# Pooled attention and Strassen feed-forward on one core: in the first unit, three copies of q of batch 1 one slot earlier, its scores and three turned parts one slot later

## The chip, the cores and the metric

The kernel runs on one core of one Trainium2 chip, all in float32. Its time is the device time of one execution in microseconds (us); of several runs the median is given. "The profile" is a page on one execution taken by the hardware profiler, and "the trace" is the record of every instruction of that execution, of which parts are shown. A chip core has five engines with a queue of instructions each, which run in order within a queue and wait for each other by semaphores: TensorE (PE in the profile, its weight loads PEld), VectorE (DVE), ScalarE (ACT), GpSimd (POOL) and SyncE (SP, which here only issues DMAs). ACT also issues a few DMAs (ACTq).

## The reference: what is computed

Two stages. First attention over 8 batches, 8 heads, 576 rows of 64, with k and v averaged over groups of 8 rows, so that there are only 72 keys:

```python
k_p = k.reshape(B, H, Sp, pool, D).mean(axis=3)
v_p = v.reshape(B, H, Sp, pool, D).mean(axis=3)
scores = scale * np.matmul(q, k_p.transpose(0, 1, 3, 2))
attn = softmax(scores)
x = (attn @ v_p), heads side by side: 4608 tokens of 512
h = x @ w_in                       # 512 -> 2048
g = h + sin(alpha * h) ** 2 / alpha
out = g @ w_out                    # 2048 -> 512
```

## The kernel before, in words

**Units and slots.** The first half of the feed-forward (x to g) is done for 9 units of 512 tokens; a batch of attention has 576 rows, so batch b+1 must be ready, in part, for unit b+1. While a unit's large products run on PE, the attention of the next batch is woven in between. `run` (L1476) calls for every unit u first `carry(u)` (L1164), which makes a dictionary from slot numbers to lists of small steps, and then `hidden(u, x)` (L814), which walks through 28 slots: four groups J = 0 to 3 of 7 slots each, k = 0 to 6. A slot issues one of the seven products of a Strassen scheme (`product`, L834; eight PE instructions on 256 columns at L842), the copies, sines and squares that go with it, and, at the place `extras()`, the steps that `carry` has put there, in the order in which they were put. No scheduler moves anything: the order of the text is the order in each engine's queue.

**What a slot of unit 0 issues** (with J its group, Q the group before):

- k = 0: last sines of Q, extras, product 1 into bank `b1`
- k = 1: ACT copies `b1` to `b6` (L818), squares of Q (L999), extras, product 5 into `b5`
- k = 2: VectorE sums of Q (`finish`, L1044), extras, product 6 into `b6`
- k = 3: store of g of Q (L1058), ACT copies `b6` to `b7` and `b5` to `p5` (L818), extras, product 2 into `b1`
- k = 4: first sines of J out of `b1` and their squares on ACT (L992, L999), extras, product 7 into `b7`
- k = 5: VectorE sum of `b7` and `p5` (L817), extras, product 3 into `b6`
- k = 6: VectorE sums (L817) and sines, extras, product 4 into `b7`

**The attention steps of batch 1 in unit 0.** q of batch 1 comes by DMA into the tile `q0`. `pairs_q` (L87) copies its five row tiles on ACT (L97) into the tile `q1`, with the heads in another order. `q_t(i)` (L279) turns row tile i: four transposes on PE (L287) into one bank and one copy out (L288), on VectorE for i = 0 and 1, on ACT for 2 to 4, into the tile `q0` again, which is free for this only when all five copies of `pairs_q` have read it. `k_t` (L271) turns the pooled keys (L276) and copies them to `kblk` on VectorE (L277). `two_scores(j)` (L301) multiplies turned q by keys (L315): for j = 0 row tiles 0 and 1, for j = 1 row tiles 2, 3 and 4; VectorE takes maximum and difference of them (`shifts`, L338 and L339), of row tile 3 and 4 only later, in slot 13 (`two_shifts`). `exp(i)` is on ACT (L364), `norm(i)` sums on VectorE (L370, L371) and multiplies on POOL (L372), `turn(i)` transposes blocks on VectorE (L499 to L509), and `move` (L512) brings the turned weights by DMA (L519) from `tr` to `aM`, of which SP issues twelve and ACT four. `all_values` (slot 26, L598) multiplies them by the pooled values. `norm_rest`, `a_rest` (L485, its copy L491) and `values_rest` (L585, L591) do the same for the last 64 rows of batch 0.

**What binds these steps besides data.** PSUM has 8 banks. Five of them (0 to 4) rotate through the groups: a group takes four, so at any time one is free, and `two_scores` uses that one, `(turn + 1) % 5`, and the banks 5, 6 and 7 beside it. The turning steps take their banks in rotation out of 5, 6 and 7 (`abank`, L772): in unit 0 the bank 6 for `q_t(0)`, 7 for `q_t(1)`, 5 for `k_t`, then 6, 7 and 5 for `q_t(2)`, `q_t(3)` and `q_t(4)`. `two_scores` puts the scores of its first row tile into the free bank and bank 7, those of the second (with those of tile 4) into banks 5 and 6. `load_q(2)` (slot 9, L69) loads batch 2 into the tile `q1`, out of which `q_t(0)` to `q_t(4)` read. Sines and exponentials need different function tables on ACT (ACT_TABLE_LOAD).

**POOL in unit 0.** `combine_w_in` (L679, adds at L683) makes the Strassen sums of the first weights for group J; `load_v(1)` (slot 7) adds up rows of v (L131) once its DMA has landed, then come `combine_w_in(2)` (slot 8), `norm(0)` and `norm(1)` (slot 10), `norm_rest` (slot 13), `norm(2)` and `norm(3)` (slot 16), `combine_w_in(3)` (slot 17).

After the 9 units, `outputs` (L1273) does the second half of the feed-forward in the same manner; nothing in it is touched.

Of the kernel before, what the change touches and what calls it, by code (L numbers as in the profile page):

```python
# [40 lines left out]
class Kernel:  # L41
# [1122 lines left out]
    def carry(self, u):  # L1164

        nc = self.nc
        x = defaultdict(list)
        at = lambda slot, f, *a: x[slot].append(lambda: f(*a))
        last = self.B - 1
        b = u + 1  # L1170
        if u == 0:
            A0, A = self.att[:2]
            at(1, A0.rest_q)
            at(1, A0.a_head, 1, (5, 6, 2))
            at(1, self.refine)
            at(2, A0.values, (2, 3), (2, 1), 1, 1)
            at(2, A0.score, 4)
            at(2, self.sums_of_x, 0, 2)
            at(2, self.sums_of_x, 0, 3)
            at(2, self.load_w_in_part, 2)  # L1180
            at(2, self.load_w_in_part, 3)
            at(2, self.pairs_q, 1, (0, 1))
            at(4, self.pairs_q, 1, (2, 3, 4))
            at(4, self.combine_w_in, 1, (0, 1, 2, 3), self.nc.gpsimd)
            at(4, A.q_t, 0, self.nc.vector.tensor_copy)
            at(4, A.q_t, 1, self.nc.vector.tensor_copy)
            at(4, A.k_t)
            at(7, self.load_v, 1)
            at(7, lambda: self.pool_v())
            for i in range(2):  # L1190
                at((5, 10)[i], A.two_scores, i)
            at(13, A.two_shifts)
            for i in range(2, 5):
                at(5 + i, A.q_t, i)
            at(9, A0.exp, 4)
            for i in range(4):
                at((9, 9, 15, 15)[i], A.exp, i)
                at((10, 10, 16, 16)[i], A.norm, i)
                at((13, 13, 19, 19)[i], A.turn, i)
            at(8, self.combine_w_in, 2, (0, 1, 2, 3), self.nc.gpsimd)  # L1200
            at(13, A0.norm_rest)
            at(17, self.combine_w_in, 3, (0, 1), self.nc.gpsimd)
            at(17, self.combine_w_in, 3, (2, 3), self.nc.gpsimd)
            at(23, A0.a_rest)
            at(24, lambda: A0.values_rest((5, 6, 7, (self.turn + 1) % 5)))
            for r in (32, 96):
                at(3, self.nc.gpsimd.memset, self.aM[r:r + 32, :, 704:736], 0.0)
            at(19, A.move, range(3))
            at(20, A.move, (3,), nc.scalar, (0,))
            at(21, A.move, (3,), nc.scalar, (1,))  # L1210
            at(26, A.all_values)
            at(9, self.load_q, 2)
            at(23, self.inner_w_in)
            for e in range(2):
                at(12, self.load_k, 2, e)
                at(17, lambda e=e: self.pool_k[e]())
            at(27, self.att[2].k_t)
            turn = 23
        else:
            at(0, self.sums_of_x, u, 2)  # L1220
            at(0, self.sums_of_x, u, 3)
        if 0 < u < last:
            A = self.att[b]
            for i in range(2):
                at((3, 5)[i], A.two_scores, i)
            at(6, A.two_shifts)
            for i in range(4):
                at((8, 9, 10, 10)[i], A.exp, i)
                at((9, 10, 11, 12)[i], A.norm, i)
                at((12, 13, 13, 13)[i], A.turn, i)  # L1230
            at(14, A.move, range(4))
            at(6, self.load_v, b)
            at(12, lambda: self.pool_v())
            for i in range(2):
                if b < last:
                    at(12, self.load_k, b + 1, i)
                    at(12, lambda i=i: self.pool_k[i]())
            at(25, A.all_values)
            if b < last:
                at(26, self.att[b + 1].k_t)  # L1240
            if 2 < u + 2 <= last:
                at(7, self.load_q, u + 2)
            at(2, self.inner_x, u)
            turn = 22
        elif u:
            turn = None
        if turn and u + 2 <= last:
            for part in range(4):
                at(((turn, turn + 1) if u == 0 else (23, 24))[part] if part < 2 else turn + part, self.turn_q, u + 2, part)
        if u + 1 < self.NU:  # L1250
            at(27, self.sums_of_x, u + 1, 0)
            at(27, self.sums_of_x, u + 1, 1)
        return x
# [336 lines left out]
```

## Time and profile before

| | |
|---|---|
| median of 3 runs (lowest to highest) | 908.77 us (908.37 to 908.81) |
| profiled execution, its own time | 905.98 us |
| its span, first to last instruction | 904.2 us |
| busy share PE, PEld, DVE, ACT, POOL | 99%, 90%, 75%, 50%, 23% |
| granted TensorE clock, mean | 0.999 |

The views that are used: the page (busy time by engine, the chain of work that ended last), the timeline of one engine (start, duration, engine, line, operation, output<-inputs, tile, xcount of merged instructions; in square brackets the idle time of the engine just before it and what ended it), the list of waits (who waited for whom: total us, times, longest) and the groups by form (mean ns of one shape). Times in a timeline are us from the span's start. Starts of merged instructions can overlap the one before, as engines are pipelined.

### The profile page before, as it was taken

The numbers are of one execution on the slowest core, as the hardware profiler recorded it, in microseconds if no ns is written. First come the engines' busy times: TensorE is split into PE (matmuls) and PEld (weight loads), VectorE is DVE, ScalarE is ACT, GpSimd is POOL, SyncE is SP. The second block draws the span as 40 slices with busy tenths as digits, with TensorE's granted clock in tenths as the row PEclk, the third lists the DMA queues.
The fourth block names the chain that finished last, engine by engine and source line by source line (L and its number), as shares of the span: only waits on it lengthen the run. The fifth ranks groups of instructions, "written<-read, shape, count | busy, mean of one in ns | idle before, by whom it ended". The sixth has DMA issues, their size and how long they took to land.

```text
span 904.2 us, 17920 instructions
## 1 busy us (share of the span) xinstructions
PE 894.7 (99%) x7002; PEld 815.3 (90%) x7002; DVE 677.6 (75%) x1012; ACT 448.6 (50%) x1072; POOL 212.1 (23%) x216
## 2 busy tenths in 40 slices
PE   9899999999999999999999999999999999999998
PEld 5687888888888888888888999999999999999997
DVE  7675766758577685764557799979798888889895
ACT  5596785877768777687976621111111111111111
POOL 5687552824438253330000000000000000000000
PEclk9999999999999999999999999999999999999999
DMA  9965866759577595648217246161618162533401
GB/s 262 246 199 148 212 175 192 193 146 277 144 208 189 167 247 138 180 132 307 85 67 239 96 135 211 47 203 40 223 27 227 36 189 74 171 92 123 141 14 40
DMA packets 128746, 141.12 MB, mean 156 GB/s; under 512 B 46920, under 2 KB 95704, under 8 KB 128664
## 3 DMA queue, kind: packets, MB, share of 16 engines
q1 hardware_dynamic: 125880, 137.88, 53.2%
q10 hardware_dynamic: 2784, 2.11, 0.9%
q8 instruction: 55, 0.90, 0.4%
q14 instruction: 27, 0.22, 0.1%
HBM read 75.37 MB, written 47.19 MB: 136 GB/s over the span
## 4 chain that ended last, share of the span: by engine, by line
PE 95%; DVE 2%; SPq 1%; ACT 1%; DMA 1%; issue 0%; DVEq 0%
PE PS L842 44%; PE PS L1323 41%; PE PS L1022 3%; PE PS L315 2%; PE PS L608 2%; SPq L677 1%; PE PS L621 1%; DVE x L1278 1%; DMA a<-in_moe_w_in_dram 1%; PE PS L1090 0%; DVE s L1278 0%; DVE r L1278 0%; PE PS L420 0%; PE PS L276 0%; SPq L101 0%
## 5 line engine op out<-in xcount | busy, mean ns | idle before, releaser
L842 PE MATMUL PS<-home,a 128*128 128x256 f32 x1104 | 257.8, 381 | 0.2
L842 PEld LDWEIGHTS PS<-home,a 128*128 128x128 f32 x1104 | 205.3, 190 | 32.6 <-issue 4.5
L842 PE MATMUL PS<-home,as 128*128 128x256 f32 x768 | 183.0, 382 | 0.0
L842 PEld LDWEIGHTS PS<-home,as 128*128 128x128 f32 x768 | 141.6, 190 | 19.8 <-ACT PS L818 1.2
L1373 POOL TENSOR_TENSOR cc<-cc,cb 128x576 f32<-128x576 f32 x1 | 2.0, 1982 | 501.8 <-DVE cb L1278 501.8
L1323 PE MATMUL PS<-s,wb 128*128 128x144 f32 x896 | 119.1, 286 | 0.0
L1323 PEld LDWEIGHTS PS<-s,wb 128*128 128x128 f32 x896 | 113.7, 190 | 0.1
L999 ACT ACTIVATE s<-s,c 128x256 f32<-128x256 f32 (+1 forms) x228 | 113.5, 564 | 0.0
L817 DVE TENSOR_TENSOR h<-PS,p 128x512 f32<-128x512 f32 x72 | 49.1, 683 | 64.4 <-PE PS L842 38.1
L131 POOL TENSOR_TENSOR kvin<-kvin 96x768 f32<-96x768 f32 (+3 forms) x42 | 74.6, 1776 | 71.4 <-DMA kvin<-in_v_dram 69.7
L1451 ACT COPY PS<-PS 128x144 f32<-128x144 f32 x56 | 14.7, 263 | 144.8 <-PE PS L1323 140.7
L992 ACT ACTIVATE s<-h,al 128x256 f32<-128x256 f32 x144 | 65.6, 509 | 41.7 <-DVE h L817 41.7
L1323 PE MATMUL PS<-r,wb 128*128 128x144 f32 x512 | 73.3, 286 | 0.3 <-DVE r L1278 0.3
L1323 PE MATMUL PS<-s,a 128*128 128x144 f32 x512 | 73.2, 286 | 0.0
L1044 DVE TENSOR_TENSOR h<-PS,s 128x512 f32<-128x512 f32 x36 | 24.7, 686 | 60.2 <-ACT s L999 60.2
L992 ACT ACTIVATE s<-PS,al 128x256 f32<-128x256 f32 x144 | 60.1, 470 | 18.7 <-PE PS L842 17.8
L1323 PEld LDWEIGHTS PS<-r,wb 128*128 128x128 f32 x512 | 67.1, 190 | 0.5 <-DVE r L1278 0.5
L1323 PEld LDWEIGHTS PS<-s,a 128*128 128x128 f32 x512 | 67.1, 190 | 0.0
L818 ACT COPY PS<-PS 128x512 f32<-128x512 f32 x72 | 41.4, 576 | 35.1 <-PE PS L842 30.3
L1471 ACT COPY PS<-PS 128x144 f32<-128x144 f32 x56 | 14.7, 263 | 88.1 <-PE PS L1323 88.1
L1323 PE MATMUL PS<-s,we 128*128 128x144 f32 x384 | 54.9, 286 | 0.0
L1323 PE MATMUL PS<-x,wb 128*128 128x144 f32 x384 | 54.9, 286 | 0.0
(216 smaller groups left out, 1406.1 us busy)
## 6 DMA issues: line engine op xcount, KB each, us to landing
g_bridge<-h SPq DMA_DIRECT2D x72, 512.0 KB
r<-g_bridge SPq DMA_DIRECT2D x31, 1152.0 KB
out_dram<-o SPq DMA_DIRECT2D x122, 72.0 KB
kvin<-in_k_dram SPq DMA_DIRECT2D x14, 576.0 KB
q<-in_q_dram SPq DMA_DIRECT2D x7, 1024.0 KB
kvin<-in_v_dram SPq DMA_DIRECT2D x14, 512.0 KB
aM<-tr SPq DMA_DIRECT2D x54, 92.0 KB
aM<-tr SPq DMA_DIRECT2D x54, 88.0 KB
```

Of the source, the lines that this page charges most:

```text
L131: self.nc.gpsimd.tensor_tensor(out=t[..., 0:w] if w > D else out, in0=t[..., 0:w], in1=t[..., w:2 * w], op=OP.add)
L315: nc.tensor.matmul(ps[e][r0 + r:r0 + r + q.shape[-1], h, :], q[s], kb[s, hp, :], start=True, stop=True)
L608: nc.tensor.matmul(o[r:r + 64], w, x, start=start and i < 2, stop=False, skip_group_check=True)
L817: add = lambda o, x, y: nc.vector.tensor_tensor(out=o, in0=x, in1=y, op=OP.add)
L818: copy = lambda o, x: nc.scalar.copy(out=o, in_=x)
L842: nc.tensor.matmul(ps[:, jj, :], self.A[p][:, kk, f * P:(f + 1) * P], x[:, kk, :], start=(start and n == 0), stop=(kk == 1), skip_group_ch ...
L992: self.nc.scalar.activation(out=G.s[:, i, jj, j, :], in_=src[:, jj], func=AF.Sin, scale=self.al[:, f:f + 1])
L999: self.nc.scalar.activation(out=x, in_=x, func=AF.Square, scale=self.c[:, f:f + 1])
L1022: nc.tensor.matmul(o, W[m][:, G.J - J0], X[m], start=start and n == 0, stop=True, skip_group_check=True)
L1044: add = lambda o, x, y: self.nc.vector.tensor_tensor(out=o, in0=x, in1=y, op=OP.add)
L1323: nc.tensor.matmul(out, W[:, J // 2, J % 2, :], A[:, J, :], start=(start and J == 0), stop=(J == self.NJ - 1), skip_group_check=True)
L1451: nc.scalar.copy(out=x1[:, 0, :], in_=x0[:, 1, :])
```

## The change

In unit 0 only, in `carry`. `pairs_q` for row tiles 2, 3 and 4 goes from slot 4 to slot 3. In slot 4 it stood behind the first sines and squares of group 0 on ACT; in slot 3 it stands behind the two copies L818 and ahead of those sines, and ahead of two memsets of POOL. `two_scores(0)` goes from slot 5 to 6 and `two_scores(1)` from 10 to 11. `q_t(2)`, `q_t(3)` and `q_t(4)` go from slots 7, 8 and 9 to 8, 9 and 10. The exponentials of row tiles 0 and 1 (slot 9), the norms (slot 10) and `load_q(2)` (slot 9) stay; so `q_t(4)` now stands behind the exponentials and behind `load_q(2)`, and the norms of tiles 0 and 1 ahead of `two_scores(1)`.

```diff
             at(2, self.pairs_q, 1, (0, 1))
-            at(4, self.pairs_q, 1, (2, 3, 4))
+            at(3, self.pairs_q, 1, (2, 3, 4))
             at(4, self.combine_w_in, 1, (0, 1, 2, 3), self.nc.gpsimd)
             at(4, A.q_t, 0, self.nc.vector.tensor_copy)
             at(4, A.q_t, 1, self.nc.vector.tensor_copy)
...
             for i in range(2):
-                at((5, 10)[i], A.two_scores, i)
+                at((6, 11)[i], A.two_scores, i)
             at(13, A.two_shifts)
             for i in range(2, 5):
-                at(5 + i, A.q_t, i)
+                at(6 + i, A.q_t, i)
             at(9, A0.exp, 4)
```

## The prediction

> **What bounds the kernel now.** I read the page first, its busy row and its chain:
>
> ```profile
> PE 894.7 (99%) x7002; PEld 815.3 (90%) x7002; DVE 677.6 (75%) x1012; ACT 448.6 (50%) x1072; POOL 212.1 (23%) x216
> ...
> PE 95%; DVE 2%; SPq 1%; ACT 1%; DMA 1%; issue 0%; DVEq 0%
> ```
>
> PE is busy for 99% of the span and carries 95% of the chain that ended last. So an edit in unit 0 gains only what PE stands idle there, and the gain lasts only if PE doesn't have to wait for something else further down. I therefore read the timeline of PE through unit 0, and then those of the engines that PE waits for. PE (start, duration, instructions, idle time before):
>
> ```profile
> 33.06 1.92 PE L842 MATMUL PS<-home,a 128*128 128x256 f32 x8
> 37.49 1.23 PE L315 MATMUL PS<-kblk,q 64*64 64x72 f32 x64 [2.51 <-DVE kblk L277]
> 38.65 1.99 PE L842 MATMUL PS<-home,as 128*128 128x256 f32 x8
> 40.48 1.89 PE L842 MATMUL PS<-home,a 128*128 128x256 f32 x8
> 42.21 0.60 PE L287 MATMUL PS<-ident,q 128*128 128x128 f32 x4
> 42.64 1.89 PE L842 MATMUL PS<-home,a 128*128 128x256 f32 x8
> 44.37 0.60 PE L287 MATMUL PS<-ident,q 128*128 128x128 f32 x4
> ...
> 46.63 0.46 PE L287 MATMUL PS<-ident,q 64*128 64x64 f32 x4
> ...
> 48.95 1.53 PE L315 MATMUL PS<-kblk,q 64*64 64x72 f32 x80
> 50.41 3.72 PE L842 MATMUL PS<-home,a 128*128 128x256 f32 x16
> ```
>
> This is slot 4 (product 7) to slots 10 and 11. One hole is there: the scores of tiles 0 and 1 (L315) stand 2.51 us behind the copy of the keys (L277, VectorE). Who holds that copy, on ACT and on VectorE:
>
> ```profile
> 30.59 0.58 ACT L818 COPY p<-PS 128x512 f32<-128x512 f32 x1
> 31.19 1.28 ACT L992 ACT_TABLE_LOAD   x1
> ...
> 33.22 0.91 ACT L999 ACTIVATE s<-s,c 128x256 f32<-128x256 f32 x2
> 34.01 1.65 ACT L97 COPY q<-q 128x512 f32<-128x512 f32 x3
> ```
>
> ```profile
> 35.69 1.29 DVE L288 COPY q<-PS 128x512 f32<-128x512 f32 x2 [4.51 <-ACT q L97]
> 36.90 0.53 DVE L277 COPY kblk<-PS 128x288 f32<-128x288 f32 x1
> 37.31 0.67 DVE L817 TENSOR_TENSOR h<-PS,p 128x512 f32<-128x512 f32 x1
> ```
>
> The three copies L97 run at 34.01, behind table load, sines and squares. VectorE's turned copies L288 write the tile that L97 reads, so they wait 4.51 us for the end of L97 at 35.66, and the keys come behind them in the queue.
>
> **The change part by part.**
>
> *The three copies in slot 3.* They start behind L818 at 31.1 instead of 34.01 and end at 32.8. L288 then runs 32.8 to 34.1 and L277 to about 34.6. The table load, sines and squares come 1.65 later: squares end at 35.8 instead of 34.13. What needs them is the last VectorE sum of slot 6, which in the new order stands behind product 3, at about 37.3; so that cover holds by 1.5 us. The loaded rows of tile 4 must have landed: the trace says only by the time they were read (L97 before 35.66). If they came as late as that, keys would come at 37.43 as before, PE would do product 3 first, and the hole would shrink to 0.9 instead of going; I take the early end, as the first two copies had no wait, and the next limits bind either way.
>
> *Scores one slot later.* Product 7 starts at 33.06; a product takes 1.73 (40.48 to 42.21, 42.64 to 44.37), 1.83 ahead of or behind the small score products. So product 3 at 34.8, scores at 36.6 (keys 34.6, turned parts 34.1: no wait), product 4 at 37.8 (37.49 to 38.65 is 1.16), product 1 at 39.6. The scores use the free bank, which product 1 of the next group takes at slot 7, now one slot nearer. VectorE must have read it; its four steps were
>
> ```profile
> 38.27 0.46 DVE L338 TENSOR_REDUCE mx<-PS 128x4 f32<-128x288 f32 x1 [0.29 <-PE PS L315]
> ...
> 40.77 0.76 DVE L339 TENSOR_TENSOR ex<-PS,mx 128x576 f32<-128x576 f32 x1
> ```
>
> 3.26 us from the first to the end of the last. New, both sums of slot 6 stand ahead of them (product 3 ends at 36.7, two sums at 0.6 spacing), so they run from 37.9 to 41.2; the free bank is read by 38.9, 0.7 ahead of product 1, and bank 6 by 41.2, when the turning of tile 2 wants it at 41.3. Price of that: 0 to 0.1. So the 2.51 hole goes nearly whole, and that is the first sum: **2.5**.
>
> *Turned parts one slot later.* On PE they cost what they did. On ACT their copies move in the queue, and tile 4 moves behind the exponentials:
>
> ```profile
> 44.57 0.57 ACT L818 COPY PS<-PS 128x512 f32<-128x512 f32 x1 [0.31 <-PE PS L842]
> ...
> 47.09 0.84 ACT L288 COPY q<-PS 128x512 f32<-128x512 f32 x2
> 47.95 1.28 ACT L364 ACT_TABLE_LOAD   x1
> ...
> 51.49 0.58 ACT L818 COPY p<-PS 128x512 f32<-128x512 f32 x1
> ```
>
> L818 at 44.57 follows product 1 by 1.93, so new at 41.5; squares end 2.52 later, 44.1; copies of tiles 2 and 3 take 1.08; the table load starts at 45.2; from it to the second L818 are 3.54 (47.95 to 51.49), so 48.7; that copy takes 0.51 up to the next start, and tile 4's copy runs 49.2 to 49.6. PE: tile 2 at 41.3, tile 3 at 43.5 (spacing 2.16), tile 4 at 45.7 (2.26), scores at 48.1 (2.32). Scores of tile 2 are 32 of 80 instructions of 1.46 us, so at 48.7 PE wants banks 5 and 6, and bank 5 still holds tile 4's turned rows until 49.6. A new wait of about **1.0**; between 0.5 (only tile 4's own scores wait) and 1.5 (all scores wait). I take 1.0, since the bank is in the code. What queues behind it is product 7, 50.6 instead of 52.14. Gain at slot 11: 2.5 - 1.0 = **1.5**.
>
> *Norms ahead of the second scores, and load_q(2).* The load must wait for tile 4's transposes, which are now behind it in the text but come on PE about 0.9 earlier than 46.63; behind it on SP stand stores and loads that PE doesn't wait for. Cost 0.
>
> *What is late next.* From slot 11 the order on all engines is as before, so all runs earlier or equal, unless held by what did not move. That is POOL, held by a DMA:
>
> ```profile
> 44.83 3.71 POOL L131 TENSOR_TENSOR kvin<-kvin 128x1024 f32<-128x1024 f32 x2 [6.47 <-DMA kvin<-in_v_dram]
> 48.61 1.60 POOL L131 TENSOR_TENSOR vm<-kvin 128x256 f32<-128x256 f32 x1
> ...
> 57.52 2.26 POOL L372 TENSOR_TENSOR ex<-ex,sm 128x576 f32<-128x576 f32 x2
> ...
> 64.52 2.83 POOL L372 TENSOR_TENSOR ex<-ex,sm 128x576 f32<-128x576 f32 x2 [0.33 <-ACT PS L818]
> ```
>
> v landed at 44.83, and POOL works without a pause from there to the end of norm 1 at 59.78. VectorE's second transposing waits for that:
>
> ```profile
> 59.97 0.67 DVE L499 STREAM_TRANSPOSE tr<-ex 128x512 f32<-128x512 f32 x1
> ...
> 66.66 0.69 DVE L817 TENSOR_TENSOR h<-PS,p 128x512 f32<-128x512 f32 x1 [1.09 <-PE PS L842]
> 67.27 0.70 DVE L499 STREAM_TRANSPOSE tr<-ex 128x512 f32<-128x512 f32 x1
> ...
> 68.08 0.67 DVE L499 STREAM_TRANSPOSE tr<-ex 128x512 f32<-128x512 f32 x1
> ```
>
> It started only 0.19 after norm 1, so this chain (last rows of batch 0 on VectorE, their norm on POOL, then norms 2 and 3) can gain 0.15 at most. Norm 3 ended at 67.35, now 67.2. VectorE, at most 1.09 earlier at L817, reaches turn 3 at 67.0 and waits: turn 3 at 67.2 instead of 68.08, a gain of **0.85**. One term goes against it. The add `vm` took 1.60 for 256 columns, where the same form on `vr` took 0.73, beside a VectorE sum with both inputs in SBUF:
>
> ```profile
> L131 POOL TENSOR_TENSOR vr<-vr 128x256 f32<-128x256 f32 x1 | 0.7, 729 | 0.0
> ```
>
> ```profile
> 47.83 1.78 DVE L1044 TENSOR_TENSOR h<-h,s 128x1024 f32<-128x1024 f32 x1
> ```
>
> So POOL lost 0.87 there. L1044 now starts at about 44.8, just where POOL starts: it may cost POOL a whole L1044, about 1.2 (1.78 less its own wait), 0.25 more than before. Turn 3 then gains 0.6. [...]
>
> Behind turn 3, ACT works without a pause: the DMA issues of slots 20 and 21, sines, squares, and the copy that the values of the last rows wait for:
>
> ```profile
> 69.46 1.51 ACTq L519 DMA_DIRECT2D aM<-tr  x2
> ...
> 72.84 0.57 ACT L818 COPY PS<-PS 128x512 f32<-128x512 f32 x1 [0.19 <-issue]
> 73.32 2.13 ACT L999 ACTIVATE s<-s,c 128x256 f32<-128x256 f32 x4
> 75.35 0.41 ACT L491 COPY last_t<-PS 128x320 f32<-128x320 f32 x1
> ```
>
> ```profile
> 75.81 0.61 PEld L591 LDWEIGHTS PS<-last_t,vm 64*64 64x64 f32 x16 [0.37 <-ACT last_t L491]
> ```
>
> PE took that copy at 75.81, as soon as it was there. Since ACT can come only as much earlier as turn 3, PE, 1.5 ahead at slot 11, waits at slots 23 and 24 until 0.6 to 0.85 are left. The twelve DMAs of SP move with turn 3, so slot 26 isn't the next hole. **Sum: 2.5 - 1.0 - 0.8 = 0.7 us.** The profiled execution has 905.98 beside its span of 904.2, so 905.3 for it; the median shown, 908.77, is 2.8 above it, and 0.7 off that is **908.1**.
>
> **The rivals.**
>
> 1. *Turn 3 doesn't hold PE* (POOL gets through sooner, or the copy L491 has more room than its row shows). Then 1.5 stay: 907.3. For: POOL lost 0.87 to one sum, and might not. Against: L591's 0.37 of idle time ends on L491.
> 2. *Neither wait appears*: the whole 2.5, 906.3. This needs tile 4's copy to be early too. Against: ACT's rows from 44.57 to 52 have no pause to win.
> 3. *Slower*: POOL's norms come later because more of its adds meet a VectorE sum, as `vm` did. Place: POOL between 44.83 and 67.35. A collision costs 0.87 to 1.25; the change moves VectorE's sums against POOL's fixed run. It decides once norm 3 ends 0.85 later than worked out; one more whole collision gives 1.2 - 0.7 = 0.5 slower, 909.2; two, 1.7, 910.4; three would pass 0.2%. For: VectorE goes up to 3 us earlier and POOL doesn't. Against: the norms at 57.52 took 1.13 each beside other VectorE steps, so few of them hurt.
>
> **How the numbers follow.** The forecast has 55%, rival 1 15%, rival 2 8%, rival 3 22%, of which 12% for more than 0.2% and 10% for a single collision. A measurement of this kernel can tell about 0.2%, 1.8 us, from no change. So faster by over that is rival 2 alone, 8%; slower 12%; within it 80%. The range leaves out rival 2 and the far part of rival 3: from 906.8, half a us below rival 1, to 909.6, rival 3 with one collision and the same margin. That also holds both ends of the waits (0.5 to 1.5) and of POOL (0.6 to 0.85).
>
> **What would show it.** Right: L97 three times at 31.1, the scores at 36.6 without a hole; at 48 to 50 a new idle time of about 1.0 inside L315, released by ACT's L288; product 7 at about 50.6; L372 at 57.5 to 57.8; turn 3 at 67.2 to 67.5; L591 at 75.0 to 75.2 with idle PE ahead of it in slots 23 and 24. Wrong: no idle time inside the second L315 (first wait), L591 at 74.3 (second), L372 after 58.7 (rival 3), or a hole left ahead of product 3.

## The result, and the profile after

| | before | after |
|---|---|---|
| median (lowest to highest), 8 executions each | 908.79 us (907.74 to 910.22) | 906.59 us (905.64 to 907.52) |
| ratio after to before, 95% interval | | 0.9973 (0.9962 to 0.9984) |
| profiled execution, its own time | 905.98 us | 905.64 us |
| its span | 904.2 us | 903.6 us |

The change makes the kernel 2.2 us faster. The range that was predicted ended at 906.8, just above the measured 906.59, and "within 0.2%" was forecast where -0.27% came. Note the two lower rows: the profiled executions are 0.34 us apart, not 2.2. Most of this study asks why the medians differ by so much more than the profiles.

The page of after, its busy row and its chain:

```profile
PE 895.2 (99%) x7002; PEld 815.8 (90%) x7002; DVE 679.4 (75%) x1012; ACT 448.7 (50%) x1072; POOL 212.2 (23%) x216
...
PE 91%; DVE 3%; ACT 2%; DMA 1%; POOL 1%; issue 1%; ACTq 0%; SPq 0%; DVEq 0%; POOLq 0%
```

PE is as busy as before, but its share of the chain has gone from 95% to 91%. The chain in order of time (start, duration, engine, output, line) shows where it leaves PE, ahead of L591:

```profile
65.95 1.64 POOL ex L372
67.61 0.71 DVE tr L499
...
72.97 2.04 ACT s L999 x4
75.37 0.75 PE PS L591 x16
```

Norm 3 on POOL, turn 3, ACT, L591: the path that the forecast named as next. PE's timeline through unit 0 (start, duration, instructions, in brackets the idle time before and its releaser):

```profile
33.75 1.92 PE L842 MATMUL PS<-home,a 128*128 128x256 f32 x8
35.51 1.89 PE L842 MATMUL PS<-home,as 128*128 128x256 f32 x8
37.33 1.23 PE L315 MATMUL PS<-kblk,q 64*64 64x72 f32 x64
38.49 3.72 PE L842 MATMUL PS<-home,a 128*128 128x256 f32 x16
...
46.49 0.46 PE L287 MATMUL PS<-ident,q 64*128 64x64 f32 x4
46.88 1.99 PE L842 MATMUL PS<-home,a 128*128 128x256 f32 x8
48.81 0.73 PE L315 MATMUL PS<-kblk,q 64*64 64x72 f32 x32
50.27 1.03 PE L315 MATMUL PS<-kblk,q 64*64 64x72 f32 x48 [0.73 <-ACT q L288]
51.23 1.56 PE L842 MATMUL PS<-home,a 128*128 128x256 f32 x6
```

Product 7 starts 0.69 later than in the profile of before (33.75 against 33.06), because the first loads landed later in this execution (POOL's first add on k starts at 8.98 instead of 8.02); so distances are compared, not clock readings. The hole of 2.51 ahead of the scores is gone. The forecast new wait is there, inside the second L315 behind its first 32 instructions and released by ACT's copy of tile 4, with 0.73 instead of 1.0. From product 7 of group 0 to product 7 of group 1 are 51.23 - 33.75 = 17.48, before 52.14 - 33.06 = 19.08: 1.6 gained, forecast 1.5.

ACT, then VectorE, in the same execution:

```profile
31.77 1.65 ACT L97 COPY q<-q 128x512 f32<-128x512 f32 x3
33.44 1.28 ACT L992 ACT_TABLE_LOAD   x1
...
49.38 0.57 ACT L818 COPY p<-PS 128x512 f32<-128x512 f32 x1
49.86 0.36 ACT L288 COPY q<-PS 128x256 f32<-128x256 f32 x1
```

```profile
33.45 1.29 DVE L288 COPY q<-PS 128x512 f32<-128x512 f32 x2 [1.59 <-ACT q L97]
34.66 0.55 DVE L277 COPY kblk<-PS 128x288 f32<-128x288 f32 x1
...
45.50 3.14 DVE L1044 TENSOR_TENSOR h<-h,s 128x1024 f32<-128x1024 f32 x1
...
60.16 0.71 DVE L499 STREAM_TRANSPOSE tr<-ex 128x512 f32<-128x512 f32 x1 [0.20 <-POOL ex L372]
...
67.61 0.71 DVE L499 STREAM_TRANSPOSE tr<-ex 128x512 f32<-128x512 f32 x1 [0.35 <-POOL ex L372]
```

The keys are there at 35.21, 2.1 ahead of PE. Turn 3 (67.61) now has idle time ahead of it that ends on POOL's norm; before there was none. POOL and the place where PE feels it:

```profile
45.20 4.57 POOL L131 TENSOR_TENSOR kvin<-kvin 128x1024 f32<-128x1024 f32 x2 [6.12 <-DMA kvin<-in_v_dram]
49.85 0.73 POOL L131 TENSOR_TENSOR vm<-kvin 128x256 f32<-128x256 f32 x1
...
57.88 2.25 POOL L372 TENSOR_TENSOR ex<-ex,sm 128x576 f32<-128x576 f32 x2
```

```profile
73.11 1.97 PE L842 MATMUL PS<-home,as 128*128 128x256 f32 x8
75.37 0.75 PE L591 MATMUL PS<-last_t,vm 64*64 64x64 f32 x16 [0.29 <-ACT last_t L491]
```

From v's landing to the end of norm 1 are 60.13 - 45.20 = 14.93 us, before 59.78 - 44.83 = 14.95: POOL's run is as long as it was, and tied to v. The collision moved from `vm` (1.60, now 0.73) into the `kvin` pair (3.71, now 4.57), where VectorE's L1044 takes 3.14 instead of 1.78. L591 comes 41.62 behind product 7, before 42.75: 1.13 of the 1.6 is left there. In absolute time L591 gained 0.44, about the 0.34 by which the profiled executions differ; against the landing of v it gained 30.98 - 30.17 = 0.81.

### The profile page after: what moved, and what is told of

It is laid out like the page before. It is cut to its first block, busy times and chain, and to the rows that moved or that the text cites. A ratio compares the mean times of both kernels' runs of the same rounds, so it can differ in the third digit from the quotient of the medians.

```text
span 903.6 us, 17919 instructions
## 1 busy us (share of the span) xinstructions
PE 895.2 (99%) x7002; PEld 815.8 (90%) x7002; DVE 679.4 (75%) x1012; ACT 448.7 (50%) x1072; POOL 212.2 (23%) x216
## 3 DMA queue, kind: packets, MB, share of 16 engines
HBM read 75.37 MB, written 47.19 MB: 136 GB/s over the span
## 4 chain that ended last, share of the span: by engine, by line
PE 91%; DVE 3%; ACT 2%; DMA 1%; POOL 1%; issue 1%; ACTq 0%; SPq 0%; DVEq 0%; POOLq 0%
PE PS L842 42%; PE PS L1323 40%; PE PS L1022 3%; PE PS L315 2%; PE PS L608 2%; DMA q<-in_q_dram 1%; PE PS L621 1%; ACT s L999 1%; POOL kvin L131 1%; DVE s L1278 1%; DMA h<-in_k_dram 1%; DVE x L1278 1%; ACT ex L364 0%; ACT s L992 0%; DVE r L1278 0%
## 5 line engine op out<-in xcount | busy, mean ns | idle before, releaser
L1044 DVE TENSOR_TENSOR h<-PS,s 128x512 f32<-128x512 f32 x36 | 24.7, 686 | 58.6 <-ACT s L999 58.6
L818 ACT COPY PS<-PS 128x512 f32<-128x512 f32 x72 | 41.5, 576 | 35.3 <-PE PS L842 30.5
```

The costliest lines, as they stand in the source:

```text
L818: copy = lambda o, x: nc.scalar.copy(out=o, in_=x)
L1044: add = lambda o, x, y: self.nc.vector.tensor_tensor(out=o, in0=x, in1=y, op=OP.add)
```

## The experiments

Each kernel ran with before beside it on the same chip. L591 serves as the mark: all steps that the change moves lie ahead of it. "At full clock" means executions whose mean granted TensorE clock is 0.999 or 1.0. The 17 profiles of this study bear this mark out: the 13 at 0.999 or 1.0 have no stretch of 3 us ahead of 900 us with a clock below 0.97, three at 0.997 have 3.4 us of half clock there and one at 0.996 has 6.8 us (experiments 6 and 8). A mean of 0.998, which many executions have, no profile shows. In the expectations, theory A is that the mechanism of the forecast holds and the gain of an execution depends on how early PE starts against v's landing (v with POOL then sets L591); theory D is that q of batch 1 usually lands later than in the profile, which widens the hole of before. Theory B is in experiment 1. Theory C is two things: in experiment 5 it is that v usually lands late; in experiments 4 (`copies_norms`) and 9, whose expectations were written after experiment 8, it is the half clock that experiment 8 shows.

**1. Both kernels again** (no edit).

> The kernel before once more, timed against itself, for the spread and for a second profile. Theory A (the change takes PE's hole ahead of the first scores, and what of it survives depends on where the loads of the start put PE against the landing of v): ratio 1.000 within 0.1%; the hole is 2.5 us again; the start of product 7 of group 0 and the landing of v differ from the first profile by up to 1 or 2 us, not by the same amount. Theory B (the two profiles show the whole gain, 0.3 to 0.6 us, and the medians differ by something outside unit 0): the same ratio, but product 7 and v lie within 0.2 us of the first profile, and the extra time of a usual execution lies behind 100 us.

> The changed kernel once more, for a second interval and a second profile. Theory A: ratio 0.997 to 0.999; from product 7 to the first product behind the second scores 1.5 to 1.6 us shorter than before; the rest of the way to the values of the last rows (L591) loses 0.3 to 0.9 of that when v lands late against PE, nothing when it lands early. Theory B: ratio 0.9995 or above here, 0.3 to 0.6 us.

Measured: before again 907.45, ratio 0.9991 (0.9976 to 1.0005); after again 905.99, 0.9974 (0.9961 to 0.9986). The result repeats. In the two profiles, 906.14 and 905.61, the hole is 2.50 and 0, the new wait 0 and 0.74, and L591 stands 42.74 behind product 7 in before, as in its first profile, and 30.20 behind v in after (30.17 in its first). So the profiles differ by some 0.5 again and the medians by 1.5 to 2.3. Product 7 (33.25) is 0.19 later than in the first profile of before and v (45.67) 0.84, so they move apart, as theory A has it. Theory B also had the extra time of a usual execution behind 100 us; experiment 8 shows it ahead of L591.

**2. The copies alone**, from before:

```diff
-            at(4, self.pairs_q, 1, (2, 3, 4))
+            at(3, self.pairs_q, 1, (2, 3, 4))
```

> The kernel before with only the three copies of q moved ahead of the first sines (slot 4 to 3); scores and turned parts in their old slots. Theory A: the hole of 2.5 goes to 0.1 or less, part 4's copy stays ahead of the exponentials, so no wait inside the second scores: 2.4 us ahead at slot 11, 0.9 more than the change; at L591 the same as the change where turn 3 holds PE, so 906 to 907 against 908.8, ratio 0.997 to 0.9985. Rival (moving the scores is what pays): ratio 1.000, the hole stays above 1.5.

Measured 906.34, 0.9972 (0.9958 to 0.9986). PE of its profile:

```profile
34.97 1.92 PE L842 MATMUL PS<-home,a 128*128 128x256 f32 x8
36.82 1.23 PE L315 MATMUL PS<-kblk,q 64*64 64x72 f32 x64
```

The scores follow product 7 without a pause, in their old slot, and L591 is 40.72 behind product 7 and 30.24 behind v. Within the interval, this single line of the diff gives the whole measured gain; what the later slots give alone is experiment 7.

**3. Tile 4 turned before the exponentials**, from after:

```diff
-                at(6 + i, A.q_t, i)
+                at((8, 9, 9)[i - 2], A.q_t, i)
```

> The changed kernel with the turned part 4 in slot 9 beside part 3, so that its copy runs ahead of the exponentials. Theory A: the idle time of 0.7 to 0.9 inside the second scores goes, the first product behind them starts 0.9 earlier (2.4 us ahead of before at slot 11); the gain at L591 stays that of the change within 0.2 where POOL's norms hold turn 3, since those don't move; ratio 0.997 to 0.999. Rival (the new wait costs its 0.9 to the end): 0.9 us faster than the change.

Measured 905.87, 0.9972 (0.9961 to 0.9984), like after. Its PE:

```profile
34.27 1.92 PE L842 MATMUL PS<-home,a 128*128 128x256 f32 x8
...
49.31 1.53 PE L315 MATMUL PS<-kblk,q 64*64 64x72 f32 x80
50.78 1.99 PE L842 MATMUL PS<-home,a 128*128 128x256 f32 x8
...
73.44 1.97 PE L842 MATMUL PS<-home,as 128*128 128x256 f32 x8 [0.79 <-ACT PS L818]
75.70 0.75 PE L591 MATMUL PS<-last_t,vm 64*64 64x64 f32 x16 [0.30 <-ACT last_t L491]
```

The new wait is gone and PE is 16.51 from product 7 to product 7, 0.97 better than after. By L591, 41.43 behind product 7 against 41.62, all but 0.19 of this is given back, in waits of 0.79 and 0.30 in slots 23 and 24 (after had only the second). L591 is again 30.27 behind v (45.43). A wait removed ahead of a later hold is worth nothing: this is the hold that the forecast described, and rival 1 falls with it for these starts.

**4. The hold taken away.** POOL's third set of Strassen sums goes behind the first norms, in before (`before_norms`), in the kernel of experiment 3 (`part4_norms`) and in that of experiment 2 (`copies_norms`):

```diff
-            at(8, self.combine_w_in, 2, (0, 1, 2, 3), self.nc.gpsimd)
+            at(11, self.combine_w_in, 2, (0, 1, 2, 3), self.nc.gpsimd)
```

> The kernel before with only POOL's weight sums for group 2 behind the norms (slot 8 to 11). Theory A: nothing to gain, since PE is the later one in it: L591 at product 7 plus 42.75 as before, ratio 1.000 within 0.1%. Rival (POOL's chain held the kernel before too): 0.998 or less.

> The changed kernel with part 4 turned in slot 9 and POOL's weight sums for group 2 moved behind the norms of tiles 0 and 1 (slot 8 to 11). Theory A: both limits go: no idle time inside the second scores, L372 at 53 instead of 58, no wait of turn on L372, L591 at product 7 plus 40.3 to 40.5 without idle PE at slots 23 and 24; ratio 0.9965 to 0.9975, the fastest so far, above all in its fastest runs (below 904.5). Rival (POOL isn't the limit): L591 stays at v plus 30.2.

> The kernel before with only the three copies of q in slot 3 and POOL's weight sums for group 2 behind the norms (slot 8 to 11); scores and turned parts in their old slots. Theories A and C: no hole, no wait inside the second scores, no hold by POOL: L591 at product 7 plus 40.2 to 40.4, ratio 0.9955 to 0.997, as the changed kernel with part 4 early and the norms first. Rival (the scores one slot later are needed for that): 0.997 or above.

Measured: before_norms 908.83, 0.9999 (0.9985 to 1.0014); part4_norms 904.85, 0.9958 (0.9945 to 0.9972); copies_norms 905.06, 0.9954 (0.9937 to 0.9971). POOL, then PE, of part4_norms, where v landed only at 46.55 and product 7 started at 33.78:

```profile
53.38 2.26 POOL L372 TENSOR_TENSOR ex<-ex,sm 128x576 f32<-128x576 f32 x2
```

```profile
73.99 0.75 PE L591 MATMUL PS<-last_t,vm 64*64 64x64 f32 x16
```

The norms come 6.8 behind v instead of 12.7, and L591 is 27.4 behind v and 40.21 behind product 7 without any idle time: 2.54 less than the 42.75 of before, which is the whole 2.51. In before itself the same edit gives nothing, since there the hole is the later limit. Its L591 is 43.42 behind product 7, not 42.75, because its hole is 3.18: the first two copies of q waited 0.62 for their load in this execution. part4_norms and copies_norms are about 4 us faster than before and, by their ratios, some 1.5 us faster than after, though the intervals overlap; moving the scores is not needed for it. In the profile of copies_norms L591 is 40.23 behind product 7, as forecast, but v landed only 8.57 behind product 7 there (11.45 in after, 12.77 in part4_norms), so it is part4_norms that tests the hold.

**5. A later start**: ten more filling products on PE in the start-up, in before and in after, to bring PE later against v:

```diff
+        fill(10)
         self.refine = refine
```

> The kernel before with ten more of its own filling products on PE at the end of the first batch (they write a bank that nothing reads), so that PE comes about 2 us later to slot 0 and the landing of v stays. Theory A (the end of unit 0 is the later of two: product 7 of group 0 plus PE's work, and v's landing plus POOL's chain): before, PE's work is 42.75 from product 7 to L591, and L591 moves with product 7, no idle PE at slots 23 and 24; ratio 1.001 to 1.0025. Theory C (the usual execution is late because v lands late): v moves by as much as product 7.

> The changed kernel with the same ten filling products. Theory A: product 7 at about 35.5 to 36, v still at 45.2 to 45.7, L591 at product 7 plus 41.15 and no idle PE at slots 23 and 24, so 1.6 us of the hole's 2.5 stay where 0.4 to 1.1 stayed in the first two profiles; against the late kernel before 0.998 to 0.9985. Rival (the second limit as the prediction had it, at all starts): L591 again 0.4 to 0.9 earlier than in the late kernel before, with idle PE at slots 23 and 24.

Measured 910.05, 1.0015 (1.0001 to 1.0029), and 906.96, 0.9979 (0.9967 to 0.9992). The two medians are 3.1 apart, more than the 2.2 without the edit and more than theory A allowed. In the profile of late_after product 7 (34.72) is late and v (44.16) early, and behind the second scores no VectorE step waits for POOL. Still L591 is 41.55 behind product 7, where theory A had 41.15, and hardly less than the 41.62 of after: PE waits 0.30 for ACT's copy L491, and ACT stood 0.84 behind a DMA of the turned weights (`aM<-tr`). So POOL is not the only thing that can make ACT late there. Against the 43.12 of late_before it is 1.57 less, but the hole of late_before is 2.87, 0.36 wider than in before; without that, 1.2 would be left. v landed late (46.54) in late_before, so the pair did not keep the distance that was meant, and neither theory is settled by it.

**6. q later**: the load of q of batch 1 behind a load of weights, in before and in after.

```diff
-        self.load_q(1)
         self.load_w_in_part(1)
+        self.load_q(1)
```

> The kernel before with q of batch 1 loaded behind the first weights of group 1 (1 MB) instead of ahead of them, so that it lands some 3 to 4 us later. Theory D (in a usual execution q lands after ACT wants to copy it, the first two copies wait, and before the change that wait goes through table load, sines, squares and the last three copies straight into the hole): the copies L97 of slot 2 wait 3 us or more on q's DMA, the hole is 2.5 plus that wait, and the time rises by 1.5 to 3.5 us, ratio 1.0015 to 1.004. Theory A alone (the hole is 2.5 us at any start): ratio 1.000, hole 2.5.

> The changed kernel with q of batch 1 loaded behind the first weights of group 1. Theory D: the same wait of 3 us or more at L97, but the keys were 2.1 us ahead of PE in the changed kernel, so a hole of about 1 us at most opens ahead of the first scores; 3.5 us or more faster than the late kernel before, ratio 0.9975 to 0.9995 against the kernel before. Theory A alone: 1.6 us faster than the late kernel before.

Measured 912.13, 1.0043 (1.003 to 1.0056), and 906.61, 0.9981 (0.9966 to 0.9996). A late q costs before some 4 us (908.02 beside it), more than the 1.5 to 3.5 of theory D, and after nothing (906.59 without the edit): after has 2.1 of room ahead of the scores. Of q_late_before, PE and then the windows (length, busy time of PE, PEld, VectorE, ACT, POOL, then granted TensorE clock, DMA share, GB/s):

```profile
40.71 2.20 PE L315 MATMUL PS<-kblk,q 64*64 64x72 f32 x64 [4.59 <-DVE kblk L277]
```

```profile
39.00:42.00 3.00, 1.29 (x44) 1.29 (x48) 2.21 (x4) 0.76 (x2) 0.00 (x0) 0.50 0.92 199
42.00:45.00 3.00, 3.00 (x37) 2.50 (x30) 2.90 (x6) 0.15 (x1) 0.62 (x1) 0.50 0.29 102
```

The hole is 4.59, and something else shows: the scores behind it take 2.20 instead of 1.23, and the granted clock is 0.50 through 6 us (6.8 with the parts of the windows of 1 us at both ends). All five executions have a mean clock of 0.996. This was the first sight of what the profile of before had not shown.

**7. The later slots alone**, from after:

```diff
-            at(3, self.pairs_q, 1, (2, 3, 4))
+            at(4, self.pairs_q, 1, (2, 3, 4))
```

> The changed kernel with the three copies back in slot 4 behind the sines: only scores and turned parts one slot later. Theories A and D: product 3 fills 1.7 us of the hole, 0.8 us (and what q is late) stay, and the wait of 0.7 to 0.9 inside the second scores stays: 0.7 to 1 us gained, ratio 0.999 to 0.9995. Rival (moving the scores is what pays): 0.9975 as the change.

Measured 906.21, 0.998 (0.9969 to 0.9991), below the 0.999 to 0.9995 of both theories, though the interval just reaches it, and near the 0.9975 of the rival. Its PE:

```profile
39.39 1.23 PE L315 MATMUL PS<-kblk,q 64*64 64x72 f32 x64 [0.79 <-DVE kblk L277]
```

With a hole of 0.79 still there, and L591 42.02 behind product 7, it is as fast as after. Neither A nor D can say why, and the rival doesn't fit experiment 2, where the scores were not moved. What it has in common with after is that 10 of 11 executions are at full clock.

**8. Another profile of before** (no edit).

> The kernel before, one more profile. Theory D: if its time is above 907.5, the copies of slot 2 wait on q's DMA (0.5 us or more) and the hole is 2.5 plus that wait; if it is near 906, no such wait and a hole of 2.5. Theory A alone: the hole is 2.5 at any time.

Its own time is 908.31, an ordinary one. The copies L97 did not wait for q, so theory D does not explain this time, though experiment 6 and the 0.62 in before_norms show that such a wait can happen. PE:

```profile
33.90 1.92 PE L842 MATMUL PS<-home,a 128*128 128x256 f32 x8
38.33 2.19 PE L315 MATMUL PS<-kblk,q 64*64 64x72 f32 x64 [2.52 <-DVE kblk L277]
40.46 2.64 PE L842 MATMUL PS<-home,as 128*128 128x256 f32 x8
42.94 1.89 PE L842 MATMUL PS<-home,a 128*128 128x256 f32 x8
```

and its windows of 1 us, with the granted clock as the third number from the right:

```profile
38.00:39.00 1.00, 0.67 (x23) 0.67 (x27) 0.83 (x2) 0.14 (x1) 1.00 (x1) 0.70 1.01 179
39.00:40.00 1.00, 1.00 (x44) 1.00 (x40) 0.40 (x1) 0.77 (x2) 0.20 (x1) 0.50 1.07 241
40.00:41.00 1.00, 1.00 (x21) 0.81 (x14) 0.93 (x4) 0.00 (x0) 0.00 (x0) 0.50 1.03 215
41.00:42.00 1.00, 1.00 (x4) 0.82 (x3) 1.00 (x2) 0.00 (x0) 0.00 (x0) 0.60 0.91 188
42.00:43.00 1.00, 1.00 (x7) 0.87 (x6) 0.83 (x2) 0.00 (x0) 0.00 (x0) 1.00 0.47 131
```

The hole is 2.52, as in the first profile. But behind it the clock is halved: read as a mix of 1.0 and 0.5, the windows hold 0.6, 1, 1 and 0.8 us of half clock, 3.4 us together. The scores and product 3 take 4.61 from 38.33 to 42.94, where the rows of before's first profile give 40.48 - 37.49 = 2.99: 1.62 lost, and L591 is 44.36 behind product 7 instead of 42.75, the same 1.61. The other 0.84 by which L591 is later than in before's first profile (78.26 against 75.81) is the start-up: product 7 at 33.90 instead of 33.06. The two spans differ by 2.3, so all the extra time lies ahead of L591.

Half clock also comes in the start-up, where the change moves nothing. The profile of copies_only (mean clock 0.997) has it; its PE, then its windows:

```profile
7.35 0.43 PE L387 MATMUL PS<-twos,home 128*128 128x64 f32 x2 [1.15 <-DVE home L164]
```

```profile
8.00:9.00 1.00, 0.92 (x31) 0.92 (x32) 0.25 (x1) 0.03 (x1) 0.02 (x1) 0.56 1.08 363
9.00:10.00 1.00, 1.00 (x16) 0.86 (x9) 0.62 (x1) 0.00 (x0) 0.92 (x2) 0.50 1.20 283
10.00:11.00 1.00, 1.00 (x7) 0.95 (x5) 0.89 (x2) 0.59 (x1) 0.51 (x1) 0.50 1.13 235
11.00:12.00 1.00, 1.00 (x34) 0.53 (x32) 0.00 (x0) 0.85 (x2) 0.82 (x2) 0.73 1.09 326
```

By the same reading these are 0.88, 1, 1 and 0.54 us, again 3.4, behind an idle PE of 1.15 (up to 7.35). The profile of copies_norms (0.997) has 3.4 us of it from 17.2 on (windows of 1 us at 0.59, 0.50, 0.50 and 0.71), behind an idle PE of 1.83 (up to 17.21), and its product 7 comes only at 37.35. So a kernel without the hole can have a drop too; one with the hole could have two, which no profile shows.

**9. The hole filled, nothing moved**: in before, ten (`fill10_before`) or five (`fill5_before`) products on constants ahead of the first scores, into the free bank. They compute nothing that is used.

```diff
+            def fill():
+                for _ in range(10):
+                    nc.tensor.matmul(self.psum([P, 4, P], (self.turn + 1) % 5), self.full[:], self.full[:].unsqueeze(1).to_broadcast([P, 4, P]), start=True, stop=True)
+            at(5, fill)
```

> The kernel before with ten filling products on PE in slot 5 ahead of the first scores (bf16, 512 columns, about 2.2 us in all, into the bank that the scores then overwrite): PE computes nothing more, but isn't idle in the hole; the keys come as late as before. Theory C (behind the hole the granted clock drops to a half for 3.4 us in two of three executions, 1.6 us each or more): scores still at product 7 plus 4.4, the share of executions with a mean clock of 0.998 or less falls from 63 of 92 to 2 in 12 or less, median 907.0 to 907.4, ratio 0.998 to 0.999. Theory D (what the medians show beyond the profile comes from loads that land late): ratio 1.000, and still executions above 909.

> The same with five filling products, about 1.1 us, so that 1.4 us of the hole stay idle. [...] Theory D: ratio 1.000.

Measured: ten 907.57, 0.9986 (0.9971 to 1.0); five 907.58, 0.999 (0.9976 to 1.0004); before beside them 908.93. PE with ten:

```profile
35.44 2.32 PE L1192 MATMUL PS<-full 128*128 128x512 bf16 x10
38.73 1.23 PE L315 MATMUL PS<-kblk,q 64*64 64x72 f32 x64 [0.97 <-DVE kblk L277]
```

The scores come no earlier than before (5.04 behind product 7 in this profile, 0.6 later than the forecast 4.4), and the kernel is still 1.4 us faster in the median: 11 of 11 executions are at full clock, against 6 of the 24 of before on the same chip. Its executions average 907.60, the 6 of before at full clock 906.90: at equal clock the filling costs 0.7, so what it gains must come from the missing drops. With five, 1.67 of idle time is left, and 7 of 12 executions are at full clock. The interval of the first reaches 1.0 and one of its executions still took 909.58, so in time this pair supports the cause rather than proving it alone; the count of clocks is the stronger evidence.

All executions with a listed clock, by the hole that the kernel's profile shows (one execution each; the single one of experiment 8 left out):

| kernel | hole, us | executions at full clock |
|---|---|---|
| after (twice), copies_only, part4_early | 0 | 40 of 44 |
| part4_norms, late_after, copies_norms | 0 | 27 of 30 |
| q_late_after | 0, but 1.00 ahead of the turning of tile 0 | 9 of 12 |
| slots_only, fill10_before | 0.79, 0.97 | 21 of 22 |
| fill5_before | 1.67 | 7 of 12 |
| before, beside the others | 2.5 | 35 of 116 |
| again_before | 2.50 | 6 of 12 |
| late_before, before_norms | 2.87, 3.18 | 9 of 24 |
| q_late_before | 4.59 | 0 of 5 |

## Why the prediction was wrong, by its own steps

- **The hole of 2.5 goes: right.** Its copies ran where they were put, the keys stood 2.1 ahead of PE.
- **A new wait of 1.0 inside the second scores: right place, 0.73.** So 1.6 instead of 1.5 was left behind slot 11.
- **POOL, tied to v, cuts it at turn 3 and L591: right.** L591 was forecast at 75.0 to 75.2 with v at 44.83; v landed 0.37 later and L591 came at 75.37. Behind product 7 the hold took 0.5 instead of 0.8, since product 7 came 0.32 nearer to v. The extra collision of 0.25 did not come, POOL's run was 14.93 against 14.95. It was an estimate, a VectorE sum that costs POOL its whole 1.2, and no run shows that term: beside L1044 POOL's `kvin` pair took 0.86 longer in after (4.57 against 3.71). Experiments 3 and 4 show the hold by having it take back 0.8 of 0.97, and by removing it; experiment 5 shows a case in which ACT was held by a DMA instead.
- **The rivals.** Rival 1 (turn 3 doesn't hold PE) and rival 2 (neither wait) gave 907.3 and 906.3; the second is near the measured time by luck, as both waits that it leaves out are in the profile. Rival 3 (more collisions on POOL) did not come.
- **The failed step: "the median shown, 908.77, is 2.8 above it, and 0.7 off that is 908.1".** It carried the distance between profile and median over, unexplained and unchanged. Behind it stands the first step, "an edit in unit 0 gains only what PE stands idle there": the hole was priced by its length, and what PE loses at half clock behind it was put at nothing. That distance was itself mostly an effect of the hole: in 81 of 116 executions of before the mean granted clock is 0.998 or lower, and these take 909.36 on average, the 35 at full clock 906.98. The profile used for the forecast, 905.98, was one of the minority. The change removes the hole and with it most of the drops: 17 of after's 20 executions are at full clock.

The sum in these terms, over these 116 executions of before and the 20 of after: at full clock 906.98 - 906.19 = 0.8, where the forecast had 0.7. Then the drop: 70% of 2.4 is 1.7 for before, 15% of 1.7 is 0.3 for after, so 1.4. Together 2.2, and the means, 908.64 and 906.45, are 2.2 apart. The forecast had the first term and not the second.

One drop behind the hole cost 1.6 in the one profile of before that shows it, while executions with a drop are 2.4 slower on average. Part of this is executions with more than one: the 65 of before at 0.997 and 0.998 are 1.9 slower than those at full clock, the 16 at 0.996 or lower 4.2, and copies_only and copies_norms show where a second drop can lie, in the start-up. That these executions have two is argued from their clock; no profile of before has two.

What stays open: the start-up alone also makes slow executions (the profile of fill5_before took 908.80 at a clock of 1.0, with product 7 at 35.59), so not all that is slower is clock. Nor is it settled what decides between a drop and none at the same hole of 2.5: the profiles of before, again_before, late_before and before_norms have the hole and keep clock 1.0 behind it.

## What to carry to other kernels

Before a difference found in one profile is taken off a median, ask why profile and median differ: list the granted clock of every execution, and if the profile is at full clock and most executions aren't, take a profile of an ordinary one. A hole of PE in an otherwise full stretch may cost more than its length: in look_before the products behind 2.52 us of it had a granted clock of 0.50 for 3.4 us and took 1.62 longer. Here closing it to less than 1 us was enough (0.79 and 0.97 left, 21 of 22 executions at full clock); with 1.67 left it was 7 of 12. A wait that is removed pays only up to the next hold, and the hold is found by tying the late marker to each candidate (here L591 to v's landing, 30.17 to 30.27 in four profiles without the hole) and seeing which distance stays constant.

## What the runs showed of the hardware

- **The clock.** Behind an idle PE the granted clock fell to 0.50 for 3.4 us in three profiles, after 2.52 (look_before), 1.83 (copies_norms) and 1.15 us (copies_only), and for 6.8 us in a fourth, within and behind 4.59 (q_late_before). The scores took 2.19 us there in look_before and 2.20 in q_late_before, 1.23 in before. Four profiles with 2.50 to 3.18 us idle show no drop, and by the mean clock 81 of 116 executions of before had one; with 0.79 (slots_only) and 0.97 us (fill10_before) idle it was one of 22 at most, with 1.00 ahead of the turning of tile 0 (q_late_after) three of 12.
- **POOL's adds beside VectorE's sum L1044** took longer by nearly the same in two places where the traces show both at once: 0.87 on `vm` in before (1.60 against 0.73, L1044 from 47.83 to 49.61) and 0.86 on the `kvin` pair in after (4.57 against 3.71, L1044 from 45.50 to 48.64). The `vr` adds in late_before took 0.99 longer (2.65 instead of 1.66, from 51.01 on); that L1044 ran beside these too is an estimate, from its start 10.34 behind the first scores in before and their 40.00 in late_before. POOL's run from v to norm 1 kept its length within 0.02 between before and after.
- **Start-up moves by more than the change is worth**: product 7 started between 33.06 and 37.35 (the latest behind a start-up at half clock) and v landed between 44.16 and 46.55 in the profiles of this study, so times read off two profiles were compared only as distances.
